# A planned attention-and-MLP kernel: fills by another rule, one conversion per weight tile, alpha of two chunks by itself

## The chip, the core and the metric

One core of a Trainium2 chip runs the whole program. It has five engines with a queue each: TensorE (PE; its weight loads are shown as PEld), VectorE (DVE), ScalarE (ACT), GpSimd (POOL) and SyncE (SP), which issues most DMAs. Each engine works through its instructions in order; semaphores hold an instruction until what it needs is done. The metric is the device time of one execution in microseconds, the median of three runs.

## The reference

```python
for t in range(S):                                   # B, H, S, D = 4, 8, 768, 48
    state = alpha[:, :, t, :, None] * state + einsum('bhd,bhe->bhde', k[:, :, t], v[:, :, t])
    y[:, :, t] = einsum('bhd,bhde->bhe', q[:, :, t], state)
x = y.transpose(0, 2, 1, 3).reshape(B * S, H * D)    # 3072 x 384
h = x @ w_in                                         # 384 x 2048, float64 words
g = h * tanh(log1p(exp(min(h, 20))))                 # h itself above 20 in the log
out = (g @ w_out).astype(float32)                    # 2048 x 384
```

## The kernel before

The sequence is cut into 24 chunks of 128 tokens (6 per batch, chunk `n` of batch `n % 4`). For each chunk, `attention(n)` forms running products of alpha by two scans on VectorE: `rest` (line 431, towards the chunk's end) and the front scan (line 443). K is multiplied by `rest`, Q by the front. TensorE then makes the scores (`sc`, line 467), VectorE masks them into `probs` (line 475), and TensorE makes the product `y` (line 490). For the state, TensorE transposes K (`kb`, line 596), ScalarE copies it (`ks`), and TensorE makes `u` (line 605). The result is split into a rounded upper and a lower part and stored in `xs`; for the first six chunks TensorE subtracts the upper part (`off`, line 522).

The MLP runs in units: a unit takes one tile of 128 of the 2048 middle columns (`f`) and 2 or 4 chunks, nine matmuls up (`h`, line 647), an activation on ScalarE and VectorE (`u`, `t`, `y`, `g`), and three matmuls down per chunk (`o`, line 711), which need `g`. Weights arrive as 64-bit words. `weight(f)` loads a tile of 768 KB (`ws`) and makes fp32 words of it on VectorE in three passes for each of its two halves: a first pass (line 311, shift and mask) and two bits passes (lines 316 and 321). ScalarE rounds the upper part (line 326); the lower is made by two TensorE matmuls (lines 343 and 344) for tiles 0 to 3, by GpSimd (line 329) for the others.

The order of the instructions is written out ahead by `Plan.order`: each task has an engine, a cost and a due time (`key`); at each step the engine takes, of its first 150 waiting tasks, the one that can begin earliest, and of equals the one with the smallest key. The instructions are then emitted in that order and never move again. Where TensorE has nothing to do at the start it runs fills: 70 matmuls on a tile of zeros, whose results nobody reads; they are tasks with the key 12.

At the end `good` is made of all checks (line 821). Only if a check fails does the general path run, a slow version of everything with loops.

Of the kernel before, what the change touches and what calls it, by code (L numbers as in the profile page):

```python
# [28 lines left out]
P = 128  # L29
# [57 lines left out]
class Plan:  # L87
# [21 lines left out]

    def order(self):  # L110
# [33 lines left out]
        while len(done) < n:  # L144
            best = None
            for e in ENGINES:
                first = None
                for t in waiting[e][:WINDOW]:
# [4 lines left out]
                    if first is None or r < first[0] - 1e-9:  # L153
                        first = (r, t)
                if first and (best is None or first[0] < best[0]):
                    best = first
            if best is None:
                raise ValueError("no task can begin: " + str([w[0].key for w in waiting.values() if w]))
            at, t = best
            e = t.engine  # L160
# [22 lines left out]
    "load part": (0.7, 3.3), "load q": (1.8, 5.0), "load v": (0.7, 4.0), "load w": (2.0, 5.0),  # L183
    "move": (0.63, 2.5), "store": (0.47, 3.0),
    "fill": (0.165, 0.2), "off": (0.4, 0.65), "w off": (0.95, 1.2), "lead": (0.27, 0.38), "bits": (0.47, 0.58), "w hi": (0.42, 0.56), "w lo": (0.95, 1.08),
# [3 lines left out]
    "scores": (1.1, 1.35), "y0": (1.1, 1.4), "y": (2.0, 2.25), "turn": (0.4, 0.65),  # L189
# [15 lines left out]
def fast_path(ctx, tc, qka, v, w, out, good):  # L205
# [73 lines left out]
    for n in reversed(range(n_chunks)):  # L279
        mine = first_unit[n] - LEAD  # L280
        due[n] = min(mine, due[n + 1] - SPREAD) if n + 1 < n_chunks else mine

# [7 lines left out]
    def weight(f):  # L290
        key = weight_unit[f] - W_LEAD
# [10 lines left out]
        fs = slice(f * P, (f + 1) * P)  # L302
        for m in range(2):
            hi, lo = (wo[:, z, f : f + 1, :] if m else wi[:, z, :, fs] for z in range(2))
            as_hi = lambda t, hi=hi: t.rearrange("p (s f) -> p s f", f=hi.shape[-1])
            lead = plan.buffer("lead")
            words = lambda z, m=m: stage.tile[:, m, :, z]

            def begin(m=m, lead=lead, words=words):
                new(lead, [P, DM], f"w_lead{f}_{m}", dtype=I32)  # L310
                nc.vector.tensor_scalar(
                    lead.tile, words(1), 3, 0x3FFFFFF8, ALU.logical_shift_left, ALU.bitwise_and
                )

            def signs(lead=lead, words=words):
                nc.vector.scalar_tensor_tensor(  # L316
                    lead.tile, words(1), -0x40000000, lead.tile, ALU.bitwise_and, ALU.bitwise_or
# [703 lines left out]
```

## Time and profile before

| | |
|---|---|
| median of 3 runs | 540.15 us (540.0 to 540.23) |
| the profiled execution | 541.82 us, its span 540.1 us |
| TensorE busy | 529.0 us (98%) |
| VectorE busy | 398.7 us (74%) |
| ScalarE busy | 398.0 us (74%) |
| GpSimd busy | 39.5 us (7%) |
| chain that ended last | PE 81%, DVE 10%, ACT 3%, DMA 3% |
| line 763, the fills | 70 matmuls, 2% of the chain |

The span is the time from the first to the last record of the profile; the execution's own time is longer by what lies around it. A share of busy time is a mean over stages with different limits. The chain follows the work back from the last instruction, at each step to what released it, or to the instruction ahead of it on its engine.

### The profile page before, as it was taken

Reading aid. Unit: us, or ns where it says so; the run is one execution under the profiler, and the core shown is the slowest. Engines: PE = TensorE matmul, PEld = TensorE weight load, DVE = VectorE, ACT = ScalarE, POOL = GpSimd, SP = SyncE. Lnnn points to the kernel's source line nnn. Section 1 sums busy time; section 2 is a strip of 40 time slices with the busy share of each in tenths; the row PEclk is TensorE's granted clock in tenths of the full one; section 3 lists DMA queues with packets and bytes.
Section 4 is the critical chain, followed back from the end, with each engine's and each line's share of the span. In section 5 each row is a group of like instructions: output and inputs, shape, how many; then the busy total and the mean of one; then the engine's idle time right before and its main releaser. Section 6 shows DMA issues by size and latency. Waiting matters only on the chain.

```text
span 540.1 us, 9382 instructions
## 1 busy us (share of the span) xinstructions
PE 529.0 (98%) x3382; PEld 466.9 (86%) x3382; DVE 398.7 (74%) x719; ACT 398.0 (74%) x910; POOL 39.5 (7%) x37
## 2 busy tenths in 40 slices
PE   8999999999999999999999999999999999999994
PEld 4778999989898888888899888889988899999994
DVE  6999999999998797668974458985457845454441
ACT  1577778898779998997967865557766567786772
POOL 2000204233342000000000000000000000000000
PEclk9999999999999999999999999999999999999998
DMA  8655626131443785466220122220032000000001
GB/s 255 189 170 175 195 75 185 64 118 59 132 170 124 233 274 182 138 207 213 74 73 2 58 74 74 74 74 2 17 110 77 13 7 1 26 34 1 1 0 64
DMA packets 21812, 54.20 MB, mean 100 GB/s; under 512 B 4000, under 2 KB 14752, under 8 KB 21760
## 3 DMA queue, kind: packets, MB, share of 16 engines
q1 hardware_dynamic: 21472, 53.45, 32.0%
q8 instruction: 28, 0.46, 0.4%
q14 instruction: 24, 0.20, 0.1%
q10 hardware_dynamic: 288, 0.10, 0.1%
HBM read 46.45 MB, written 4.72 MB: 95 GB/s over the span
## 4 chain that ended last, share of the span: by engine, by line
PE 81%; DVE 10%; ACT 3%; DMA 3%; issue 1%; SPq 0%; ACTq 0%; DVEq 0%
PE o L711 31%; PE h L647 31%; PE y L490 7%; PE sc L467 4%; PE u L605 3%; PE spare L763 2%; DVE t L674 2%; PE kb L596 2%; DMA wc<-in_wp_dram 1%; DVE g L681 1%; DMA qka<-in_qka_dram 1%; DVE y L665 1%; DVE w_lead L316 1%; DVE w_lead L321 1%; DVE rest L431 1%
## 5 line engine op out<-in xcount | busy, mean ns | idle before, releaser
L711 PE MATMUL o<-wo,g 128*128 128x384 f32 x1152 | 227.2, 342 | 0.3 <-DVE g L681 0.3
L647 PE MATMUL h<-xs,wi 128*128 128x512 f32 (+1 forms) x954 | 218.7, 374 | 0.6 <-POOL wi L329 0.3
L711 PEld LDWEIGHTS o<-wo,g 128*128 128x128 f32 x1152 | 202.0, 188 | 9.6 <-issue 1.0
L647 PEld LDWEIGHTS h<-xs,wi 128*128 128x128 f32 x954 | 166.8, 188 | 28.0 <-POOL wi L329 0.8
L655 ACT ACTIVATE u<-h 128x512 f32<-128x512 f32 (+1 forms) x106 | 58.6, 552 | 80.9 <-PE h L647 80.2
L681 DVE TENSOR_TENSOR g<-t,g 128x512 fp32r<-128x512 f32 (+1 forms) x106 | 68.1, 643 | 49.5 <-ACT g L678 49.1
L665 DVE SCALAR_TENSOR_TENSOR y<-u,h 128x512 f32<-128x512 f32 (+1 forms) x106 | 67.0, 633 | 49.4 <-ACT u L655 48.9
L674 DVE SCALAR_TENSOR_TENSOR t<-y,t 128x512 f32<-128x512 f32 (+1 forms) x106 | 69.5, 657 | 9.3 <-ACT t L671 9.0
L668 ACT ACTIVATE t<-t,tenth 128x512 f32<-128x512 f32 (+1 forms) x106 | 71.8, 677 | 2.0
L678 ACT ACTIVATE g<-t 128x512 fp32r<-128x512 f32 (+1 forms) x106 | 61.7, 583 | 9.8 <-DVE t L674 5.1
L661 ACT ACTIVATE t<-u 128x512 f32<-128x512 f32 (+1 forms) x106 | 62.5, 589 | 3.1 <-DVE g L681 0.6
L671 ACT ACTIVATE t<-t 128x512 f32<-128x512 f32 (+1 forms) x106 | 61.6, 581 | 0.7
L431 DVE TENSOR_TENSOR_SCAN rest<-qka,behind 112x516 f32<-112x516 f32 x24 | 30.9, 1286 | 9.6 <-DMA qka<-in_qka_dram 9.5
L475 DVE COPY_PREDICATED probs<-causal,sc 128x512 f32<-128x512 uint32 x48 | 33.1, 731 | 3.5 <-PE sc L467 3.4
L443 DVE TENSOR_TENSOR_SCAN qka<-qka,ahead 112x516 f32<-112x516 f32 x24 | 30.8, 1282 | 0.0
L467 PEld LDWEIGHTS sc<-qka 48*128 48x128 f32 x384 | 23.3, 187 | 6.7 <-issue 4.5
L329 POOL TENSOR_TENSOR wi<-w_lead,wi 128x384 fp32r<-128x384 f32 x12 | 19.8, 1651 | 114.6 <-ACT wi L326 114.6
L467 PE MATMUL sc<-qka 48*128 48x128 f32 x384 | 27.9, 285 | 0.0
L490 PE MATMUL y<-probs,v 128*64 128x128 f32 (+1 forms) x384 | 26.1, 278 | 0.0
L490 PEld LDWEIGHTS y<-probs,v 128*64 128x64 f32 (+1 forms) x384 | 20.3, 129 | 3.8 <-issue 0.7
L490 PEld LDWEIGHTS y<-qka,state 112*112 112x112 f32 x160 | 19.9, 176 | 1.8 <-DVE probs L475 0.5
L490 PE MATMUL y<-qka,state 112*112 112x128 f32 x160 | 20.9, 273 | 0.2 <-DVE probs L475 0.2
(83 smaller groups left out, 401.3 us busy)
## 6 DMA issues: line engine op xcount, KB each, us to landing
qka<-in_qka_dram SPq DMA_DIRECT2D x23, 674.2 KB, 5.1
ws<-in_wp_dram SPq DMA_DIRECT2D x16, 768.0 KB, 4.5
wc<-in_wp_dram SPq DMA_DIRECT2D x16, 768.0 KB, 4.7
v<-in_vp_dram SPq DMA_DIRECT2D x24, 192.0 KB, 3.3
out_dram<-osb SPq DMA_DIRECT2D x16, 192.0 KB, 1.9
xs<-x SPq DMA_DIRECT2D x138, 16.0 KB, 2.9
out_dram<-part SPq DMA_DIRECT2D x8, 192.0 KB, 2.7
qka<-in_qka_dram SPq DMA_DIRECT2D x2, 224.0 KB, 3.6
```

The lines of the kernel that those rows point to most:

```text
L467: nc.tensor.matmul(p[a][:, j], K()[r : r + D, j], Q()[r : r + D, j], start=True, stop=True)
L490: nc.tensor.matmul(o, l, r, start=m < (2 if first else 1), stop=m >= len(ops) - 2, skip_group_check=True,)
L647: nc.tensor.matmul(p[:, :N], wi[:, z, s, fs], x[:, a, s], start=m == 0, stop=m == len(passes) - 1)
L655: nc.scalar.activation(wide(u), wide(h), AF.Exp, scale=-1.0, accum_out=uchk[:, at : at + 1])
L661: nc.scalar.activation(wide(t), wide(u), AF.Square, bias=1.0, scale=2.0)
L665: nc.vector.scalar_tensor_tensor(wide(y), wide(u), 0.5, wide(h), ALU.add, ALU.mult)
L668: nc.scalar.activation(wide(t), wide(t), AF.Ln, bias=tenth, scale=0.1)
L671: nc.scalar.activation(wide(t), wide(t), AF.Exp, scale=-1.0)
L674: nc.vector.scalar_tensor_tensor(wide(t), wide(y), 0.4, wide(t), ALU.mult, ALU.mult)
L678: nc.scalar.activation(g.tile[:, 0, :N], wide(t), AF.Copy)
L681: nc.vector.tensor_tensor(g.tile[:, 1, :N], wide(t), g.tile[:, 0, :N].bitcast(F32), ALU.subtract)
L711: nc.tensor.matmul(o.tile, g.tile[:, a, j * C : (j + 1) * C], wo[:, z, f], start=begins and m == 0, stop=end and m == 2,)
```

## The change

The two halves of a weight tile are converted together: three VectorE passes of 768 columns instead of six of 384, in one buffer `lead` of twice the size. The rounding and the lower parts stay as two halves. For chunk 1, alpha is loaded by itself, one planned microsecond ahead of q and k, which come in one transfer; chunk 0 has three parts as before. The fills read the identity matrix instead of a zeroed tile. A fill is now planned only where TensorE would otherwise wait for longer than one lasts, and only up to a planned time of 26; what is left is dropped. Of 150, 56 are emitted (before: 70 of 70). They stand in runs: before 22 (to `kb` of chunk 0), 9 (to its scores), 12 (to its product), 6, 2, 6, 2, 10 and 1; now 10, 12, 11, 5, 2, 2, 3, 3 and 8. Some planned costs are new, and two tables of shifts are there, empty. In the general path the loop over the middle columns takes four tiles at a time and loads their weights anew for each 128 rows.

```diff
-FILLS = 70
-FILL_KEY = 12.0
+FILLS = 150
+IDLE, IDLE_UNTIL, IDLE_BANK = 12.34567, 26.0, "o3"
+PARTED = 2
+DUE_SHIFT = {}
+W_SHIFT = {}
-W_PE = 4
+W_PE = lambda f, m: f < 4
+STOP_AT = 1e9
...
-                    if first is None or r < first[0] - 1e-9:
+                    if t.key == IDLE:
+                        spare = spare or (r, t)
+                    elif first is None or r < first[0] - 1e-9:
                         first = (r, t)
+                if spare and spare[0] > IDLE_UNTIL:
+                    dropped = self.drop(waiting, free_slots)
+                elif spare and (first is None or first[0] > spare[0] + spare[1].cost):
+                    first = spare
...
-    "fill": (0.165, 0.2), "off": (0.4, 0.65), "w off": (0.95, 1.2), "lead": (0.27, 0.38), "bits": (0.47, 0.58), "w hi": (0.42, 0.56), "w lo": (0.95, 1.08),
+    "fill": (0.165, 0.2), "fill0": (0.33, 0.36),
+    "off": (0.34, 0.6), "w off": (0.84, 1.08), "lead": (0.47, 0.58), "bits": (0.87, 0.98),
...
+        lead = plan.buffer("lead")
+        words = lambda z: stage.tile[:, :, :, z]
+        def begin():
+            new(lead, [P, 2, DM], f"w_lead{f}", dtype=I32)
+            nc.vector.tensor_scalar(
+                lead.tile, words(1), 3, 0x3FFFFFF8, ALU.logical_shift_left, ALU.bitwise_and
+            )
...
+        bits = add("DVE", *COST["lead"], key, begin, [got], [stage, lead], port=True)
+        bits = add("DVE", *COST["bits"], key + 0.01, signs, [bits], [stage, lead], port=True)
+        bits = add("DVE", *COST["bits"], key + 0.02, ends, [bits], [stage, lead], port=True)
         for m in range(2):
...
-            t = add("DVE", *COST["lead"], k, begin, [got], [stage, lead], port=True)
-            t = add("DVE", *COST["bits"], k + 0.01, signs, [t], [stage, lead], port=True)
-            t = add("DVE", *COST["bits"], k + 0.02, ends, [t], [stage, lead], port=True)
-            a = add("ACT", *COST["w hi"], k + 0.03, upper, [t], [lead])
+            a = add("ACT", *COST["w hi"], k + 0.03, upper, [bits], [lead])
...
+        elif n < PARTED:
+            got_a, got_k = (
+                add("SP", *COST[z], key - Q_LEAD - early, load_part(*e), uses=[q_buf])
+                for z, e, early in (
+                    ("load part", (a_at, QKA), 1.0), ("load two", (0, a_at), 0.0)
+                )
+            )
+            got_q = got_k
...
-        nothing = const.tile([P, DM], BF16, name="nothing")
-        nc.vector.memset(nothing, 0.0)
+        some = ident.bitcast(BF16)[:, :P]
...
-            nc.tensor.matmul(spare.tile[:, :DM], nothing[:, :P], nothing, start=True, stop=True)
+            nc.tensor.matmul(
+                spare.tile[:, :DM].rearrange("p (j t) -> p j t", j=NK), some,
+                some.unsqueeze(1).broadcast_to([P, NK, P]), start=True, stop=True,
+            )
         for i in range(FILLS):
-            add("PE", *COST["fill"], FILL_KEY if i else -1e6, fill, uses=[spare])
+            cost = COST["fill" if i > 12 else "fill0"]
+            add("PE", *cost, IDLE if i else -1e6, fill, uses=[spare])
...
-            for f0 in range(0, NFF, 4):
+            with tc.For_i(0, NFF, 4) as f0:
+                wi = sb.tile([P, NK, 4 * P], F32, name="wi_g")
+                wo = sb.tile([P, 4, DM], F32, name="wo_g")
```

On SyncE, the transfers at the start, before: `qka_115` and `v_122` are chunk 0, `qka_129` and `v_144` chunk 1, `ws` the weight tiles 0 and 1.

```order
L409 DMA qka_115<-in_qka_dram 112x517
L409 DMA qka_115<-in_qka_dram 112x512 x2
L413 DMA v_122<-in_vp_dram 128x384
L404 DMA qka_129<-in_qka_dram 112x1541
L413 DMA v_144<-in_vp_dram 128x384
L296 DMA ws_153<-in_wp_dram 128x1536
L296 DMA ws_173<-in_wp_dram 128x1536
L404 DMA qka_217<-in_qka_dram 112x1541
```

The same place now: chunk 0 is `qka_113`, chunk 1 `qka_119`.

```order
L441 DMA qka_113<-in_qka_dram 112x517
L441 DMA qka_113<-in_qka_dram 112x512 x2
L441 DMA qka_119<-in_qka_dram 112x517
L445 DMA v_124<-in_vp_dram 128x384
L441 DMA qka_119<-in_qka_dram 112x1024
L445 DMA v_136<-in_vp_dram 128x384
L328 DMA ws_145<-in_wp_dram 128x1536
L328 DMA ws_159<-in_wp_dram 128x1536
L436 DMA qka_220<-in_qka_dram 112x1541
```

Alpha of chunk 1 stands ahead of the v of chunk 0, its q and k in the place of the whole transfer.

On VectorE, from the front scan of chunk 0 to the front scan of chunk 1, before (`rest_185` is the scan of chunk 1, line 475 the masks of chunk 0):

```order
L443 SCALAR_TENSOR_TENSOR qka_115<-qka_115,ahead 112x516
L453 TENSOR_TENSOR qka_115<-qka_115 112x512
L431 SCALAR_TENSOR_TENSOR rest_185<-qka_129,behind 112x516
L475 COPY_PREDICATED probs_91<-causal,sc_0_175 128x512
L475 COPY_PREDICATED probs_93<-causal,sc_1_176 128x512
L436 RECIPROCAL ahead<-rest_185 112x4
L439 TENSOR_TENSOR qka_129<-qka_129,rest_185 112x512
L443 SCALAR_TENSOR_TENSOR qka_129<-qka_129,ahead 112x516
```

The same now (`rest_151` is the scan of chunk 1, line 515 the masks of chunk 0):

```order
L483 SCALAR_TENSOR_TENSOR qka_113<-qka_113,ahead 112x516
L471 SCALAR_TENSOR_TENSOR rest_151<-qka_119,behind 112x516
L493 TENSOR_TENSOR qka_113<-qka_113 112x512
L476 RECIPROCAL ahead<-rest_151 112x4
L479 TENSOR_TENSOR qka_119<-qka_119,rest_151 112x512
L483 SCALAR_TENSOR_TENSOR qka_119<-qka_119,ahead 112x516
L515 COPY_PREDICATED probs_91<-causal,sc_0_169 128x512
L515 COPY_PREDICATED probs_93<-causal,sc_1_170 128x512
```

The scan of chunk 1 has moved ahead of the multiplication of q of chunk 0, and three more passes of chunk 1 ahead of the masks of chunk 0.

On VectorE, from the end of that stretch to the scan of chunk 2, before (`ws_153` is weight tile 0, `rest_286` the scan of chunk 2):

```order
L311 TENSOR_SCALAR w_lead_0_222<-ws_153 128x384
L453 TENSOR_TENSOR qka_129<-qka_129 112x512
L316 SCALAR_TENSOR_TENSOR w_lead_0_222<-ws_153,w_lead_0_222 128x384
L311 TENSOR_SCALAR w_lead_1_245<-ws_153 128x384
L321 SCALAR_TENSOR_TENSOR w_lead_0_222<-ws_153,w_lead_0_222 128x384
L316 SCALAR_TENSOR_TENSOR w_lead_1_245<-ws_153,w_lead_1_245 128x384
L475 COPY_PREDICATED probs_91<-causal,sc_0_234 128x512
L475 COPY_PREDICATED probs_93<-causal,sc_1_235 128x512
L321 SCALAR_TENSOR_TENSOR w_lead_1_245<-ws_153,w_lead_1_245 128x384
L431 SCALAR_TENSOR_TENSOR rest_286<-qka_217,behind 112x516
```

The same now (`ws_145` and `ws_159` are weight tiles 0 and 1, `rest_274` the scan of chunk 2):

```order
L493 TENSOR_TENSOR qka_119<-qka_119 112x512
L340 TENSOR_SCALAR w_lead_204<-ws_145 128x768
L340 TENSOR_SCALAR w_lead_206<-ws_159 128x768
L345 SCALAR_TENSOR_TENSOR w_lead_204<-ws_145,w_lead_204 128x768
L345 SCALAR_TENSOR_TENSOR w_lead_206<-ws_159,w_lead_206 128x768
L515 COPY_PREDICATED probs_91<-causal,sc_0_208 128x512
L515 COPY_PREDICATED probs_93<-causal,sc_1_209 128x512
L350 SCALAR_TENSOR_TENSOR w_lead_204<-ws_145,w_lead_204 128x768
L350 SCALAR_TENSOR_TENSOR w_lead_206<-ws_159,w_lead_206 128x768
L471 SCALAR_TENSOR_TENSOR rest_274<-qka_220,behind 112x516
```

Two whole weight tiles are converted ahead of the scan of chunk 2, where it was one.

## Rows read from the trace of the kernel before

**Rows 1.** Busy time by stretches: length, engines (instructions), granted clock, DMA share, GB/s.

```profile
0.00:10.00 10.00, 7.55 (x31) 4.03 (x32) 7.12 (x15) 2.09 (x4) 3.52 (x13) 1.00 0.82 227
...
35.00:60.00 25.00, 25.00 (x221) 22.04 (x220) 24.79 (x55) 20.54 (x60) 2.40 (x1) 1.00 0.59 176
...
100.00:165.00 65.00, 64.42 (x351) 57.46 (x350) 64.66 (x113) 54.37 (x116) 22.28 (x16) 1.00 0.33 110
```

**Rows 2.** Chain of waits, 0 to 30 us: start us, us, what.

```profile
2.45 6.57 PE spare L763 x22
...
9.41 1.46 PE spare L763 x9
...
11.96 2.06 PE spare L763 x12
...
15.04 1.08 PE spare L763 x6
...
16.39 0.34 PE spare L763 x2
...
18.78 0.98 PE spare L763 x6
```

**Rows 3.** Instructions in order of time, TensorE: start us, us, what, idle before.

```profile
2.45 6.57 PE L763 MATMUL spare<-nothing 128*128 128x384 bf16 x22 [2.45 <-DVE behind L240]
```

**Rows 4.** In order of time, weight loads of TensorE, 2 to 9 us.

```profile
2.74 0.15 PEld L763 LDWEIGHTS <-nothing 128*128 128x128 bf16 x1 [0.17 <-issue]
...
8.18 0.45 PEld L763 LDWEIGHTS <-nothing 128*128 128x128 bf16 x3 [0.17 <-issue]
```

**Rows 5.** In order of time, ScalarE.

```profile
2.72 0.31 ACT L230 ACTIVATE minus_ident<-ident 128x128 fp32r<-128x128 f32 x1 [0.62 <-POOL ident masks.py:199]
```

**Rows 6.** In order of time, VectorE, chunks 0, 1 and 3.

```profile
5.64 0.66 DVE L439 TENSOR_TENSOR qka<-qka,rest 112x512 f32<-112x512 f32 x1
...
7.48 0.69 DVE L453 TENSOR_TENSOR qka<-qka 112x512 f32<-112x512 f32 x1
9.37 1.23 DVE L431 TENSOR_TENSOR_SCAN rest<-qka,behind 112x516 f32<-112x516 f32 x1 [1.20 <-DMA qka<-in_qka_dram]
...
27.94 1.23 DVE L431 TENSOR_TENSOR_SCAN rest<-qka,behind 112x516 f32<-112x516 f32 x1 [1.09 <-DMA qka<-in_qka_dram]
```

**Rows 7.** DMA issues, 2.15 to 2.6 and 4 to 5 us: count, KB each, us to landing.

```profile
v<-in_vp_dram SPq DMA_DIRECT2D x1, 192.0 KB, 4.4
...
ws<-in_wp_dram SPq DMA_DIRECT2D x2, 768.0 KB, 8.7
```

**Rows 8.** In order of time, TensorE, products of chunks 0, 1 and 2.

```profile
13.95 1.09 PE L490 MATMUL y<-probs,v 128*64 128x128 f32 x16
...
19.68 1.09 PE L490 MATMUL y<-probs,v 128*64 128x128 f32 x16
...
27.95 1.09 PE L490 MATMUL y<-probs,v 128*64 128x128 f32 x16
```

**Rows 9.** In order of time, VectorE, passes of a weight tile.

```profile
23.95 0.35 DVE L311 TENSOR_SCALAR w_lead<-ws 128x384 int32<-128x384 int32 x1
24.21 0.55 DVE L321 SCALAR_TENSOR_TENSOR w_lead<-ws,w_lead 128x384 int32<-128x384 int32 x1
24.69 0.55 DVE L316 SCALAR_TENSOR_TENSOR w_lead<-ws,w_lead 128x384 int32<-128x384 int32 x1
```

**Rows 10.** Groups by shape, VectorE, 0 to 100 us: count, busy, mean ns, idle before.

```profile
L665 DVE SCALAR_TENSOR_TENSOR y<-u,h 128x256 f32<-128x256 f32 x20 | 8.3, 417 | 1.4 <-ACT u L655 1.1
```

**Rows 11.** In order of time, VectorE, the same line at double width.

```profile
525.40 0.69 DVE L665 SCALAR_TENSOR_TENSOR y<-u,h 128x512 f32<-128x512 f32 x1 [0.95 <-ACT u L655]
```

**Rows 12.** Chain of waits, 80 to 170 us: first and last VectorE pieces of a stretch.

```profile
88.03 0.43 DVE g L681
...
135.86 0.60 DVE g L681
```

**Rows 13.** In order of time, VectorE, the last row.

```profile
533.78 0.15 DVE L821 TENSOR_REDUCE good<-pf 1x1 int32<-1x7 f32 x1 [0.38 <-PE pf L820]
```

More of the change, by code (lines that the diff above doesn't have):

```diff
@@ L108, in add, with drop @@
         return t
+    def drop(self, waiting, free_slots):
+        left = [t for t in waiting["PE"] if t.key == IDLE]
+        waiting["PE"] = [t for t in waiting["PE"] if t.key != IDLE]
+        for t in left:
+            for u in t.uses:
+                u.left -= 1
+                if u.left == 0:
+                    free_slots[u.tag].append(u.free_at)
+                    free_slots[u.tag].sort()
+        return len(left)
     def order(self):
@@ L144, in order @@
         while len(done) < n:
-            best = None
+            best, dropped = None, 0
             for e in ENGINES:
-                first = None
+                first = spare = None
                 for t in waiting[e][:WINDOW]:
@@ L281, in fast_path @@
         due[n] = min(mine, due[n + 1] - SPREAD) if n + 1 < n_chunks else mine
+    for n, shift in DUE_SHIFT.items():
+        due[n] += shift
     ready_w = {}
     def weight(f):
-        key = weight_unit[f] - W_LEAD
+        key = weight_unit[f] - W_LEAD + W_SHIFT.get(f, 0.0)
         stage = plan.buffer("stage")
@@ L320, in ends @@
-            def ends(lead=lead, words=words):
-                nc.vector.scalar_tensor_tensor(
-                    lead.tile, words(0), 29, lead.tile, ALU.logical_shift_right, ALU.bitwise_or
-                )
-            def upper(lead=lead, hi=hi, as_hi=as_hi):
-                nc.scalar.activation(hi, as_hi(lead.tile.bitcast(F32)), AF.Copy)
-            def lower(lead=lead, hi=hi, lo=lo, as_hi=as_hi):
-                nc.gpsimd.tensor_tensor(
-                    lo, as_hi(lead.tile.bitcast(F32)), hi.bitcast(F32), ALU.subtract
-                )
@@ L342, in off @@
                     p = new(bank, [P, NPAIR * C], f"w{f}_{m}", ps)[:, :DM]
-                    nc.tensor.matmul(p, ident, lead.tile.bitcast(F32), start=True, stop=False)
+                    nc.tensor.matmul(p, ident, both(), start=True, stop=False)
                     nc.tensor.matmul(as_hi(p), minus_ident, hi, start=False, stop=True)
@@ L547, in attention @@
         last_front = t_front
-        t_k = add("DVE", *COST["mult"], key + 0.03, mult_k, [t_rest, got_k], [q_buf, rest], port=True)
+        t_k = add(
+            "DVE", *COST["mult"], key + 0.03, mult_k, [t_rest, got_k], [q_buf, rest], port=True
+        )
         t_q = add("DVE", *COST["mult"], key + 0.04, mult_q, [t_front, got_q], [q_buf], port=True)
@@ L923, in general_path @@
                 nc.vector.tensor_tensor(t, ph, t, ALU.mult)
+                po = ps.tile([P, DM], F32, name="po_g")
                 for i in range(4):
                     nc.tensor.matmul(
[L926 removed]
+                        po, t[:, i], wo[:, i], start=i == 0, stop=i == 3
                     )
[L928 to L929 removed]
+                nc.vector.tensor_tensor(o, po, o, ALU.add)
             nc.sync.dma_start(out[ds(r0, P), :], o)
```

67 lines of the change are left out of this document (36 added, 31 removed).

## The prediction

> **What bounds the kernel now.** I read the busy time by stretches first. From 35 us on TensorE is busy in every microsecond: 25.00 of 25.00 us, and still 64.42 of 65.00 us in the stretch in which VectorE is busiest (64.66) [rows 1]. Every useful matmul before has its counterpart after, so from there on the time is a fixed amount of TensorE work. What a change can give or take lies where TensorE does no useful work, which is nearly all ahead of 31 us. There the chain of waits shows it running the fills (`spare`, line 763) in six runs between the first attention steps [rows 2], and the start of the first fill shows 2.45 us of idle ahead of it [rows 3]. So I add up what is not useful before, do the same for the changed order, and take the difference.
>
> **Before.** Idle 2.45 us [rows 3]. The six runs of the chain are 6.57 + 1.46 + 2.06 + 1.08 + 0.34 + 0.98 = 12.49 us for 57 fills [rows 2]; 70 are issued in all (line 60). The 35 of the last five runs take 5.92 us, 0.169 us each, so the other 13 cost 13 x 0.169 = 2.20 us. Together 17.14 us.
>
> Why were the first 22 so long? Their weight loads start 0.32 us apart from 2.74 to 8.18 us; then three stand within 0.45 us [rows 4]. A fill moves 384 columns, and 384 in 0.32 us is 1.2 per ns: the lower of the two clock levels, although the granted clock reads 1.00 in the first 10 us too [rows 1]. 18 fills ran so, from 2.45 to about 8.2 us.
>
> **The change, part by part.**
>
> *The fills' operand.* The memset of `nothing` (line 758) goes; the fill reads `ident`, and ScalarE, which waits for the same tile from GpSimd, starts at 2.72 us [rows 5]. TensorE then begins at about 2.75 instead of 2.45: idle +0.30. The memset's place on VectorE saves nothing, since the cast behind it waits for GpSimd's mask. The same 384 columns pass.
>
> *The count and places of the fills.* Ahead of the first key transpose (`kb`) stand 10 fills where 22 stood, then 12 (9 before) up to the first scores, 11 (12) up to the first product, then 5, 2, 2, 3, 3 and 8: 56 in all. Ten at 0.32 end at 2.75 + 3.20 = 5.95. The transposes need the multiplication by `rest`, 5.64 + 0.66 = 6.30 [rows 6]: a wait of about 0.38. At the lower clock they take twice their 0.39 (the gap between 9.02 and 9.41 in [rows 2]), to 7.1: another 0.39. If the clock rises as before, at 8.2 to 8.4, four more fills run at 0.32 and the remaining 42 at 0.169. Not useful after: 2.75 + 3.20 + 0.38 + 0.39 + 1.28 + 7.10 = 15.10 us. I add 0.3 us for waits that the next parts leave, 15.4.
>
> *Alpha alone for chunk 1.* VectorE has stood idle for 1.20 us until the whole qka of chunk 1 landed, and scanned from 9.37 [rows 6]. Now alpha is the fourth transfer, in the place of v, which was issued at about 2.2 and took 4.4 us for 192 KB [rows 7]. For 226 KB I take 4.4 to 5.2 and so 6.6 to 7.4. The front scan of chunk 0 ends at 7.48 [rows 6], so this scan starts there, 1.9 us sooner. It stands ahead of the multiplication of q of chunk 0, which moves from 7.48 to about 8.73 and ends at 9.4; the scores of chunk 0, which wait for it, are not reached before 7.1 + 1.28 + 8 x 0.169 = 9.75 anyway, so it costs nothing while those fills stand there. The other part of chunk 1, a later issue behind the same bytes, should land at 9.4 to 9.9; then k (0.58) and the front scan (1.2) end at 11.2 to 11.7, the scores at 9.75 + 1.09 = 10.84, and the two masks at 12.5 to 12.9. The product of chunk 0 starts when 11 fills are through, 10.84 + 1.86 = 12.7, not 13.95 [rows 8]. SyncE gains one issue; its later issues are unchanged in order but for v, and move by about 0.45 us.
>
> *One conversion for both halves.* Six VectorE passes per weight tile become three of double width. Starts 0.26 behind a first pass and 0.48 behind a bits pass [rows 9] make 2 x (0.26 + 0.48 + 0.48) = 2.44 us a tile. Of the wide passes no row exists. Ends: at the least nothing beyond today's narrow passes (half, 1.22 us), at the most the full double, 2.44. I take a value near the double: `y` on VectorE takes 0.417 us for 256 elements and 0.69 for 512 [rows 10, 11], 1.07 ns per element, so 0.41 of the 0.48 us goes by the elements and 0.07 is fixed. Saving 0.07 of each pair gives 0.46 + 0.89 + 0.89 = 2.24, a saving of 0.2 a tile, 3.2 for 16. While TensorE is full this is worth nothing. But from 88 to 137 us nearly all pieces of the chain are VectorE's, passes of the weights among them [rows 12]: there VectorE must come forward by as much as TensorE, or the lead is lost. What moves is the order. After the q of chunk 1 (13.1) stand the first passes of two weight tiles and then the second passes: 0.46 + 0.46 + 0.89 + 0.89, with the second tile's load behind one more transfer (8.7 us at the median of the two [rows 7], the later one near 14.0). So the masks of chunk 1 run from 16.2 to 17.4, and its product follows at 17.5 (before 19.68 [rows 8]). Two third passes (1.78) end at 19.2, the scans of chunk 2 follow, its q at about 22.8, its scores on TensorE at 23.2 behind what stands there, its product at about 26.6. Before, that product started at 27.95 [rows 8]. In the stretch that follows the weight matmuls stand earlier by one group of 0.9 us, so the lead grows from 1.35 to about 1.9, near to what the sum gives. VectorE comes forward by more: its scan of chunk 3, at 27.94 before after 1.09 us of idle [rows 6], stands at about 26.9, with one narrow pass (0.48) and two wide ones (1.35) more behind it, 2.8 us of lead, and 0.2 a tile from there. So it holds in 88 to 137 us.
>
> *Without cost.* The new cost figures act through the order alone; the two shift tables are empty, the stop time is far away, and tiles 0 to 3 are still split on TensorE. The general path runs only if a check fails, and no row of its lines is in the trace. It still is code to be jumped over: between the last reduction, 533.78 + 0.15, and the end at 540.1 lie 6.2 us [rows 13]. No row shows the jump. As ends I take one transfer saved or added, 4.4 us at the most by the v of [rows 7], likelier under 2, and as value zero, since the long loops over VectorE stay.
>
> **The sum.** 17.14 - 15.4 = 1.74, and of the 0.58 us of idle in 100 to 165 us [rows 1], where VectorE now has the lead, I take 0.4 as gone: 2.14 us. The profiled execution took 541.82 us for a span of 540.1 us, 1.67 above the median of 540.15; its time would be 539.68, and the median 538.0.
>
> **A rule against this.** The row first: the slow fills last until 8.18, with TensorE busy from 2.45 [rows 4]. The Trainium skill (TensorE: Matmul & The Clock Gate, Part 1) states that the half clock is the default, that sustained activity releases it, and that the moment varies from run to run. The trace agrees that the first fills run at the half clock; whether a start at 2.75 with a gap at 5.95 delays the release no run here shows. By the rule it could come later than I assume; the second of the rivals prices this by rows.
>
> **The rivals.** *The convoy on VectorE.* With two tiles' passes ahead of the masks of chunk 1, a load that lands at 15.6 instead of 14.0 holds the masks up by 1.6 us; the product of chunk 1 is then at 19.1, and the gain of 2.14 shrinks to 0.5: 539.6, no change to speak of. For it: the load is the last of eight at the start, the slowest kind [rows 7]. Against it: VectorE arrives there only at 13.5.
>
> *The clock rises late.* If it stays low until 15.5 us, the scores of chunk 0 begin at 7.1 + 12 x 0.32 = 10.9 and last 2.2, seven fills run at 0.32 and four at 0.169, and the product is at 16.1, 2.1 later than before (13.95). Masks and products of chunk 1 follow at 20.6 (before 19.68), and with six more fills on the way to chunk 2 than there were, the end is 1.2 us late: 541.4. It decides from about 13 us. Against it: the three runs lie within 0.23 us of each other, so the rise does not wander much.
>
> *Long passes ahead of the gates.* From 88 to 137 us VectorE is the chain that ended last [rows 12]. A bits pass that is 0.40 us longer can hold up a gate step and so the matmuls that need it. If each of the eight tiles converted there held TensorE twice by 0.40, that is 6.4 us: 540.15 - 2.14 + 6.4 = 544.4, slower. It decides where TensorE's stock of ready matmuls is under 0.40 us; with half of the 16 at that, 541.2. Against it: 0.58 us of idle in 65 us says that the stock is nearly always there, and VectorE starts the stretch 2.8 us ahead.
>
> *The change does not do what it says:* fewer fills only bring back plain waits of the same length, since TensorE waits for the same scans. Then the loss before 31 us stays 17 us, and 540.1 results. Against it: the 1.20 us of idle on VectorE is real, and masks now wait for scans that begin 1.9 us sooner.
>
> **How the numbers follow.** My forecast with gains of 1.1 to 3.1 us (the upper end: no wait at all and the idle of the middle gone): 0.72. Convoy 0.10 and no effect 0.06, both within 0.2%, that is 1.08 us either way, what a measurement can tell. The late clock 0.04 and the long passes 0.08, slower in most of their cases. That is faster 0.72, same 0.17, slower 0.11. The forecast's own range is 537.0 to 539.1. Eight times in ten needs the convoy too, and below it a part of what the jump may save: 536.6 to 539.9.
>
> **What the new profile would show.** First fill at 2.75; ten slow ones; first scores near 9.8 and product near 12.7; the scan of chunk 1 near 7.5 with no wait for its load; the product of chunk 1 near 17.5 and of chunk 2 near 26.6; weight passes near 0.5 and 0.95 us each; TensorE full from 35 us. I am wrong if the fills stay slow past 10 us, if a wait for a weight load stands ahead of the masks of chunk 1, or if TensorE's idle between 60 and 300 us grows beyond 1.5 us.

## The result and the profile after

The changed kernel takes 544.52 us (median of 9 runs, 543.08 to 547.06), the kernel before 540.23 (9 runs beside them). The ratio is 1.0068, 95% interval 1.0049 to 1.0086: slower by 0.7%. The forecast of 538.0 and its range were wrong, and so was its sign. The profiled execution took 543.66 us for a span of 541.7.

In the profiled execution it went as forecast ahead of 31 us. TensorE in order of time (start us, us, what, idle before), against [rows 3, 8]:

```profile
2.74 3.38 PE L804 MATMUL spare<-ident 128*128 128x384 bf16 x10 [2.74 <-POOL ident masks.py:199]
6.36 0.99 PE L638 MATMUL kb<-ident,qka 112*128 112x112 f32 x4 [0.24 <-DVE qka L479]
7.16 2.13 PE L804 MATMUL spare<-ident 128*128 128x384 bf16 x12
...
12.21 1.10 PE L530 MATMUL y<-probs,v 128*64 128x128 f32 x16
...
16.89 1.09 PE L530 MATMUL y<-probs,v 128*64 128x128 f32 x16
...
26.13 1.09 PE L530 MATMUL y<-probs,v 128*64 128x128 f32 x16
```

Ten fills at the lower clock level, then the products of chunks 0, 1 and 2 at 12.21, 16.89 and 26.13 instead of 13.95, 19.68 and 27.95. But TensorE has no longer its full work behind that. Busy time by stretches, columns as in [rows 1], and the middle stretch of the kernel before as the last line:

```profile
35.00:60.00 25.00, 24.34 (x216) 21.45 (x215) 24.04 (x46) 17.85 (x57) 2.02 (x2) 1.00 0.53 162
60.00:100.00 40.00, 38.98 (x309) 36.47 (x309) 38.99 (x79) 33.19 (x102) 9.52 (x7) 1.00 0.44 135
100.00:165.00 65.00, 64.14 (x349) 57.43 (x348) 61.83 (x89) 55.13 (x121) 24.51 (x16) 1.00 0.37 123
...
60.00:100.00 40.00, 39.79 (x316) 37.61 (x315) 38.16 (x86) 32.09 (x100) 9.92 (x8) 1.00 0.43 126
```

TensorE is idle for 0.66 + 1.02 + 0.86 = 2.54 us between 35 and 165 us; before, 0.00 + 0.21 + 0.58 = 0.79. To see where the lead went I weighed every useful matmul by the usual distance from its start to the next and added them up to a given time. Against a second profile of the kernel before, the changed kernel is ahead by about 1.3 us at 35, 0.5 at 60 and 0.2 at 80; behind by 0.8 at 90, 1.4 at 120, 1.0 at 165 and 2.4 at 530.

**Where it is lost, first place: the moves of x of chunk 2.** SyncE's issues in order of time (`ws` a weight tile, `xs<-x` the moves, the first `ws` is tile 3, the second tile 4), and two lines of the kernel before, the moves and tile 4 behind them:

```profile
26.23 0.33 SPq L328 DMA_DIRECT2D ws<-in_wp_dram  x1
27.82 0.33 SPq L436 DMA_DIRECT2D qka<-in_qka_dram  x1
28.46 0.33 SPq L328 DMA_DIRECT2D ws<-in_wp_dram  x1
30.56 3.88 SPq L576 DMA_DIRECT2D xs<-x  x6
...
32.72 4.50 SPq L536 DMA_DIRECT2D xs<-x  x6
...
37.94 0.38 SPq L296 DMA_DIRECT2D ws<-in_wp_dram  x1
```

The tile whose load stood behind the moves before (37.94 us there) now stands ahead of them. DMA issues of the moves (count, KB each, median us to landing), now and before, and what ScalarE then waits for:

```profile
xs<-x SPq DMA_DIRECT2D x6, 16.0 KB, 6.3
...
xs<-x SPq DMA_DIRECT2D x6, 16.0 KB, 3.9
```

```profile
39.05 0.28 ACT L548 ACTIVATE x<-y 112x128 fp32r<-112x128 f32 x1 [1.06 <-DMA xs<-x]
```

A move of 16 KB takes 6.3 us to land (the six took 3.9 before), ScalarE stands 1.06 us, and TensorE loses 0.6 us there in this execution.

**Second place: gate pieces behind a weight pass that GpSimd holds up.** VectorE from 114 us, then GpSimd, ScalarE and TensorE at the same time:

```profile
114.57 1.37 DVE L340 TENSOR_SCALAR w_lead<-ws 128x768 int32<-128x768 int32 x1
115.87 0.34 DVE L498 TENSOR_TENSOR state<-state,rest 48x192 f32<-48x192 f32 x1
116.14 0.94 DVE L345 SCALAR_TENSOR_TENSOR w_lead<-ws,w_lead 128x768 int32<-128x768 int32 x1
117.00 0.68 DVE L723 TENSOR_TENSOR g<-t,g 128x512 fp32r<-128x512 f32 x1
```

```profile
114.06 1.47 POOL L366 TENSOR_TENSOR wo<-w_lead,wo 128x384 fp32r<-128x384 f32 x1
```

```profile
114.74 0.63 ACT L720 ACTIVATE g<-t 128x512 fp32r<-128x512 f32 x1 [0.43 <-DVE t L716]
```

```profile
117.74 0.44 PE L753 MATMUL o<-wo,g 128*128 128x384 f32 x1 [0.86 <-DVE g L723]
```

ScalarE has the upper half of the gate ready at 115.4. VectorE's lower half (L723) stands behind two passes of a weight tile and a small piece. The first pass takes 1.37 us, while the median for this line is 0.55: it started while GpSimd subtracted, and it ends 0.4 us after the subtraction does (115.94 and 115.53). So the gate piece starts at 117.0 and TensorE stands for 0.86 us. At 87.4 us the same happens behind a pass of 1.77 us:

```profile
85.22 1.77 DVE L345 SCALAR_TENSOR_TENSOR w_lead<-ws,w_lead 128x768 int32<-128x768 int32 x1
...
87.38 0.97 PE L753 MATMUL o<-wo,g 128*128 128x384 f32 x4 [0.50 <-DVE g L723]
```

The Trainium skill (SBUF — State Buffer, SBUF: two separate sides) states that VectorE and GpSimd share one pair of ports to the on-chip memory SBUF, and that whichever of a GpSimd instruction and a VectorE instruction of certain kinds (two inputs from SBUF, or a mode that uses both ports) starts first holds the pair to its end. The trace agrees: 43 VectorE pieces start during a subtraction, and 15 of them come out over 0.25 us longer, the longest by 0.85; none of the nine `y` pieces among the 43 does, whose input `h` is TensorE's output and not in SBUF. That the ports are the reason is what the skill states; the runs below show that the long pieces come and go with the subtractions. Over the whole kernel (min/median/max ns, first and last start):

```profile
L345 DVE SCALAR_TENSOR_TENSOR w_lead<-ws,w_lead x16: 933/950/1770, 13.7 to 147.6; 128x768 int32<-128x768 int32 x16
```

Between 35 and 166 us there are 15 VectorE pieces that took over 0.25 us more than the median of their kind, with 10.1 us more in all, each beside a subtraction. In both profiles of before it is 13 pieces with 9.4 us, each beside one too. The sum of the holds is hardly new; what stands behind them is.

**Third place: the end.** The last VectorE row:

```profile
534.74 0.15 DVE L866 TENSOR_REDUCE good<-pf 1x1 int32<-1x7 f32 x1 [0.38 <-PE pf L865]
```

From the end of this reduction to the end of the span it is 541.7 - (534.74 + 0.15) = 6.8 us; before it was 6.2 [rows 13].

### The profile page after: what moved, and what is told of

It reads as the page before. It is cut to its first block, busy times and chain, and to the rows that moved or that the text cites. A ratio compares the mean times of both kernels' runs of the same rounds, so it can differ in the third digit from the quotient of the medians.

```text
span 541.7 us, 9312 instructions
## 1 busy us (share of the span) xinstructions
PE 527.5 (97%) x3368; PEld 465.6 (86%) x3368; DVE 395.5 (73%) x670; ACT 397.0 (73%) x910; POOL 39.6 (7%) x37
## 4 chain that ended last, share of the span: by engine, by line
PE 79%; DVE 12%; ACT 3%; DMA 3%; issue 2%; SPq 1%; POOL 0%; DVEq 0%; ACTq 0%; POOLq 0%
PE o L753 33%; PE h L689 31%; PE y L530 6%; PE sc L507 4%; PE u L647 2%; DMA ws<-in_wp_dram 2%; DVE w_lead L345 1%; DVE probs L515 1%; PE kb L638 1%; DVE t L716 1%; DVE g L723 1%; DVE y L707 1%; DMA xs<-x 1%; PE spare L804 1%; DVE rest L471 1%
## 5 line engine op out<-in xcount | busy, mean ns | idle before, releaser
L723 DVE TENSOR_TENSOR g<-t,g 128x512 fp32r<-128x512 f32 (+1 forms) x106 | 68.4, 646 | 53.0 <-ACT g L720 52.5
L471 DVE TENSOR_TENSOR_SCAN rest<-qka,behind 112x516 f32<-112x516 f32 x24 | 29.5, 1231 | 12.7 <-DMA qka<-in_qka_dram 12.7
L483 DVE TENSOR_TENSOR_SCAN qka<-qka,ahead 112x516 f32<-112x516 f32 x24 | 29.7, 1236 | 0.0
```

The lines of the kernel that those rows point to most:

```text
L723: nc.vector.tensor_tensor(g.tile[:, 1, :N], wide(t), g.tile[:, 0, :N].bitcast(F32), ALU.subtract)
```

## The experiments

Ratios are to the kernel before, run beside it on the same chip. One thing holds for all of these runs: an edit that changes a task of the plan lets the planner write a new order, so that more may differ than the lines shown. Where the traces show that the order stayed, it is said.

**Undoing and doing parts.** Narrow passes back (the changed kernel with the conversion of before):

```diff
-lead.tile, words(1)  # 128x768, three passes a tile
+lead.tile, words(1)  # 128x384, three passes a half, own buffer and due time
```

> The changed kernel with the six narrow passes per weight tile back (fills, alpha and general path stay changed). Theory of the double-width passes (they stand ahead of gate steps on VectorE and bring weight loads forward): the 4 us lost go and the early lead of about 2 us stays, 538 to 539.5 us. Theory of the code that is jumped over or of the fills: still 543 to 545 us.

541.45 us, 1.0004 (0.9992 to 1.0017), between the two ranges that were expected. The loss is in the double-width conversion and the order that comes with it; but the rest gives no gain either.

The conversion alone, in the kernel before (the zero operand of the fills cut to 128 columns, read three times, to make room):

```diff
-COST lead 0.27, bits 0.47; six passes of 128x384
+COST lead 0.47, bits 0.87; three passes of 128x768
```

> The kernel before with only the conversion in one piece of double width (the zero tile of the fills is cut to 128 columns and read three times, for space). Theory of the double-width passes: 542.5 to 545 us, TensorE's idle between 35 and 165 us above 2 us (before: 0.8). Theory that the fills or the code cost the time: 539 to 540.5 us.

546.86 us, 1.0111 (1.0090 to 1.0132), more than the 542.5 to 545 expected. TensorE is idle for 1.85 us from 60 to 100 and 1.64 from 100 to 165, and for 2.20 us from 20 to 35 as well, where in the two profiles of before it was 0.19 and 0.74.

The general path alone, in the kernel before:

```diff
-for f0 in range(0, NFF, 4):
+with tc.For_i(0, NFF, 4) as f0:  # and the loads of wi, wo inside
```

> The kernel before with only the general path changed, which does not run. Theory of the jumped-over code: 540.9 to 541.5 us, with all of the growth between the last reduction and the end and outside the span (before: 6.2 and 1.7 us). Every other theory: 540.2 us, unchanged.

541.52 us, 1.0007 (0.9994 to 1.0019): not told from nothing by the time; but in its profile 7.1 us follow the last reduction. The order on VectorE, ScalarE and TensorE is that of before.

**The loads.** Tiles 4 and 5 of the changed kernel loaded behind the moves of x of chunks 2 and 4:

```diff
+w_load[4].behind += moves[2]
+w_load[5].behind += moves[4]
```

> The changed kernel with the loads of weight tiles 4 and 5 held behind the x moves of chunks 2 and 4, where they stood before. Theory that the early load of tile 4 delays these moves (7.5 us instead of 2.9), so ScalarE and then the gates, and that VectorE never makes it up: 541 to 542.5 us, x moves of chunk 2 landing in under 4 us, no wait of ScalarE for them. Theory that the order of the passes on VectorE costs it by itself: 543.5 to 545 us although the moves land early.

543.25 us, 1.0043 (1.0023 to 1.0063): about a third of the loss, between the two ranges expected and with an interval that overlaps the changed kernel's. The moves land in 3.5 us and ScalarE doesn't wait for them. But of the 670 VectorE instructions only 556 stand in the same sequence as in the changed kernel, so the load is not the only difference.

**Pass length or joint readiness.** Six narrow passes in the changed kernel's task; each half rounded after its own three, or both after all six:

```diff
-upper, [bits], [lead]
+upper, [halves[m]], [lead]   # split_half
+upper, halves, [lead]        # split_joint
```

> The changed kernel with the six half-width VectorE passes put back into its new task: they write the two halves of the one double-width buffer, and ScalarE's rounding of each half waits for the three passes of its own half. Buffers and keys stay as the change has them. Theory 1, pass length (a gate piece that becomes ready behind a 0.56 or 0.94 us pass waits longer than behind a 0.35 or 0.55 us one): the loss goes, 541.0 to 542.2 us, as with all of the conversion put back (541.45). Theory 2, half readiness (the upper and lower weight halves of a tile reach ScalarE, GpSimd and TensorE only when the whole tile has been converted): also 541.0 to 542.2. Theory 3, the loads (the single double-width buffer and one key for both halves bring the conversion and its loads forward into the moves of x): 543.5 to 545. TensorE idle 60 to 100 us 1.0 us or more under theory 3, under 0.8 under the others.

> As split_half, but the rounding of either half waits for all six passes of the tile. Theory 1, pass length: 541.0 to 542.2 us. Theory 2, half readiness: 543.5 to 545, as the changed kernel. Theory 3, the loads: 543.5 to 545 as well, and here weight tile 4 is issued ahead of the moves of x of chunk 2, as in the changed kernel. Only theory 1 has this one fast; split_half fast beside it slow speaks for theory 2.

541.96 us, 1.0025 (1.0007 to 1.0044), and 544.42 us, 1.0068 (1.0045 to 1.0091). Taken alone, that speaks for joint readiness and against the length of a pass. But the second also has the load of tile 4 ahead of the moves, as said, and pays for it. Its waits from 35 to 60 us (us, times, longest):

```profile
ACT x L555 <- DMA xs<-x: 5.4, 1, 5.4
```

So this pair doesn't part the two. The first has a stall of TensorE on a gate piece too (1.2 us at 117), narrow as its passes are.

Due times of tiles 4 to 15 later by two units:

```diff
-W_SHIFT = {}
+W_SHIFT = {f: 2.0 for f in range(4, NFF)}
```

> The changed kernel with the planner's due times of weight tiles 4 to 15 later by two units (a unit of the schedule is one ScalarE piece of the gates), so that the wide passes and their loads stand behind gate pieces that they stood ahead of; weight tile 4 is still loaded ahead of the moves of x of chunk 2. Theory 1, pass length: the passes are as long as before and as many, 543.5 to 545 us. Theory 2, half readiness: later weights make it worse, 544 to 546. Theory 3 in the form that conversion stands too early among the gates (it ends at 150 us and not at 165): 541.5 to 542.7.

543.10 us, 1.0042 (1.0025 to 1.0058); the stalls at 86 and 117 us stay. None of the three theories said 543.1. As a test of the due times it is weak: 663 of the 670 VectorE instructions stand in the same sequence as in the changed kernel. It does bear on the loads: tile 4 is still loaded ahead of the moves, which land in 5.2 us, but ScalarE doesn't wait for them, TensorE is not idle from 35 to 60 us, and the run is as far below the changed kernel as the one with the loads held.

A second profile of the kernel before:

> The kernel before, unchanged, for a second profile of it. If the clock's rise differs between executions, the first 22 fills take about 5.3 us here and the budget of time that is not useful comes to some 16 us, 1.2 less than the 17.14 us of the first profile; if it doesn't, the fills take 6.6 us again. The end from the last reduction to the end of the span, 6.2 us in the first profile: within 0.3 of that if the 0.6 to 0.9 us that the changed general path showed is its own, up to 7 if it is spread of the runs.

540.27 us. Its 22 first fills:

```profile
2.45 5.40 PE L763 MATMUL spare<-nothing 128*128 128x384 bf16 x22 [2.45 <-DVE behind L240]
```

5.40 us, not the 6.57 of [rows 2]. The fills stand 0.32 us apart up to about 5.8 us and 0.16 from there, where in the first profile that step came at 8.2: the clock rose 2.4 us sooner, which made the 22 fills 1.2 us shorter. The end took 6.2 us again.

**Wide only ahead of the gates, or only among them.**

```diff
+WIDE = lambda f: f < 4    # mixed; mixed_rev: f >= 4
```

> The changed kernel with the double-width conversion for weight tiles 0 to 3 alone (they are converted before the gates start); tiles 4 to 15 are converted as before, six narrow passes, each half with a buffer and due time of its own. Theory 1, the loss sits in the conversion among the gates (tiles 4 on) and the gain in the one ahead of them: the lead of TensorE's useful work that the changed kernel had at 35 to 50 us (1.35 us over the second profile of the kernel before) is kept, 539.5 to 541.0 us, at or just under the kernel before. Theory 2, any new order draws a few stalls of its own, wherever the wide passes are: 541.5 to 543.5. Theory 3, the wide conversion of the first tiles (weight loads crowding the moves of x) costs as well: over 542, with TensorE idle 20 to 60 us of 0.6 us or more.

> The reverse: narrow conversion for tiles 0 to 3, double width for tiles 4 to 15. Theory 1 (the loss sits in tiles 4 on): 543.5 to 545.5 us, as the changed kernel or worse, with the stalls of TensorE on gate pieces between 60 and 165 us. Theory 2 (any new order): 541.5 to 543.5, no different from the mixed kernel. Theory 3 (the first tiles): 541.0 to 542.

543.96 us, 1.0055 (1.0035 to 1.0074), and 544.87, 1.0081 (1.0057 to 1.0104). My theory 1 fell: the first was to be as fast as before; its time is in the range of theory 3, that the wide conversion of the first tiles costs as well. It again loads tile 4 ahead of the moves (ScalarE waits 1.13 us) and waits 0.7 us for one gate piece; the second waits 2.0 us in three places for the same line.

**Without the subtractions.** GpSimd's 24 subtractions for tiles 4 to 15 go, in both kernels; the low halves are read from tile f mod 4:

```diff
-b = add("POOL", *COST["w lo"], k + 0.04, lower, [a], [lead], port=True)
+b = a
-wo[:, z, f]
+wo[:, z, f % 4 if z else f]   # wi alike
```

> The changed kernel without GpSimd's 24 subtractions of tiles 4 to 15; where the products want the low half of such a tile they read that of tile f mod 4, so TensorE has the same instructions but the output is another. Fourteen to sixteen VectorE pieces between 35 and 166 us are some 0.7 us longer while a subtraction runs, 10 us in all, with or without the change. Theory P, the loss is made where such a stretched piece and a wide one stand together ahead of a gate piece: without the subtractions the two stalls at 87 and 117 us go and the loss with them, 539.5 to 541.5 us, and at most 0.1% above the kernel before that also lacks them. Theory Q, the loss comes from the order and the joint readiness alone: still 2.5 to 4 us above that kernel.

> The kernel before without the same 24 subtractions, as the partner of the run just above. TensorE is hardly idle in it between 35 and 300 us (0.8 us in its second profile), so there is little for it to gain: 539.5 to 541.2 us under either theory.

Changed 539.23 us, 0.9970 (0.9953 to 0.9987); before 539.56 us, 0.9973 (0.9955 to 0.9991). The difference of 0.7% is gone. But the order is another in both: of the changed kernel's 670 VectorE instructions 559 stand in the same sequence as with the subtractions, of the 719 before 549. So this pair shows that the wide passes can go without loss, not yet that the subtractions alone made it. The changed kernel without them, by stretches and for the same line of VectorE:

```profile
60.00:100.00 40.00, 39.92 (x319) 38.14 (x318) 39.63 (x86) 34.41 (x105) 0.00 (x0) 1.00 0.51 158
100.00:165.00 65.00, 65.00 (x355) 58.38 (x354) 53.10 (x85) 62.84 (x137) 0.00 (x0) 1.00 0.48 160
```

```profile
L345 DVE SCALAR_TENSOR_TENSOR w_lead<-ws,w_lead x16: 936/950/957, 15.7 to 130.4; 128x768 int32<-128x768 int32 x16
```

The wide passes are as many, and as long at the median, and in this order they cost TensorE nothing: the longest takes 0.957 us, not 1.77. TensorE's idle time falls from 1.88 to 0.08 us in these two stretches, VectorE's work from 100 to 165 by 8.7.

That run also made the low halves ready sooner. So the same with all of the work kept, each subtraction cut in three. The plan is the same here, and so is the order of all VectorE and ScalarE instructions in both kernels:

```diff
-nc.gpsimd.tensor_tensor(lo, lead, hi, ALU.subtract)      # 128x384
+for a, b in cuts: nc.gpsimd.tensor_tensor(lo[:, a, b], ...)  # 128x128
```

> The changed kernel with each of GpSimd's subtractions (128x384, 1.0 to 1.2 us at the least) issued as three of 128x128, in the same place; the order on all engines is otherwise the same and TensorE waits for the low halves as before. Theory P (the loss is made by VectorE pieces that wait while a subtraction runs): if the hold lasts as long as one GpSimd instruction, a stretched piece gets 0.2 to 0.4 us longer instead of 0.7, and the time comes to 540.5 to 542.5 us; the sum of the stretches between 35 and 166 us falls from 10 us to under 7. If the third instruction is held as long as the whole was, or each cut pays a fixed price, 544 to 546. Theory R (without the subtractions the low halves were ready sooner, and that alone gave the gain): the cuts change nothing, 543.5 to 545, even where the stretches fall.

> The kernel before with the same three cuts. Its TensorE is idle little, so under theory P it gains less than the changed kernel: 539.5 to 541.0 us. If each cut pays a fixed price: 541.5 to 543. Theory R: no change, 540.5 to 541.5.

Changed 543.05 us, 1.0038 (1.0021 to 1.0055); before 540.43, 0.9986 (0.9961 to 1.0010). The changed kernel by stretches:

```profile
60.00:100.00 40.00, 39.61 (x324) 36.70 (x323) 39.15 (x79) 32.88 (x100) 13.91 (x20) 1.00 0.50 152
100.00:165.00 65.00, 64.90 (x354) 58.01 (x354) 62.47 (x94) 56.81 (x126) 39.82 (x48) 1.00 0.37 124
```

Idle 0.49 us instead of 1.88, and the stretched pieces cost 6.4 us instead of 10.1. In the changed kernel TensorE waits for gate pieces twice in these stretches (us in all, times, longest):

```profile
PE o L753 <- DVE g L723: 1.4, 2, 0.9
```

With the cuts, in the same order, it waits for none. The low halves don't come sooner either: GpSimd is busy for 53.7 us from 60 to 165 us, not 34.0. So it is the length of the hold that makes the waits at 87 and 117 us (theory P), and neither the order alone nor early low halves. The time shows less: it lies between the two ranges, 1.5 us under the changed kernel, and the two intervals still overlap. The profiled execution took 544.66 us and came to 60 us 2.5 us behind that of the changed kernel, which by itself gives VectorE more room; the pair with the loads held, below, has the same result from starts 0.6 us apart.

**What is left.** Both remedies at once, without and with the subtractions:

> The changed kernel without GpSimd's 24 subtractions (low halves of tiles 4 to 15 read from tile f mod 4) and with the loads of weight tiles 4 and 5 issued behind the moves of x of chunks 2 and 4. If the two causes, the load ahead of the moves and the VectorE pieces stretched by the subtractions, are the whole loss, the early gain of the change is left: 1.0 to 1.5 us below the kernel before without subtractions (539.56), 538.0 to 538.6 us. If the load costs nothing by itself: 539.0 to 539.5, as without the hold (539.23). If the change has no gain of its own: 539.3 to 540.

> The changed kernel complete, with both remedies: the loads of weight tiles 4 and 5 behind the moves of x, and each subtraction issued as three of 128x128. By the sum of the two measured alone (-1.3 and -1.4 us from 544.5): 541.5 to 542.2 us. If the remedies meet the same stalls: 542.8 to 543.3. If the stretches are all that is left beside the early gain: 540.0 to 541.0, at the kernel before.

539.50 us, 0.9983 (0.9967 to 0.9999), and 541.81, 1.0025 (1.0008 to 1.0042). The remedies add up, as expected of the second. Its order is that of the run with the loads held and whole subtractions (543.25); TensorE's idle time from 60 to 165 us falls from 1.55 to 0.20 us between the two, and the time by 1.4. But without subtractions holding the loads gives nothing (539.23 without the hold), and the first shows no gain of the change's own, though TensorE is not idle at all from 35 to 300 us. Its last VectorE row, under the line that gives the span:

```profile
core 0 of [0], span 537.9 us
...
531.12 0.15 DVE L871 TENSOR_REDUCE good<-pf 1x1 int32<-1x7 f32 x1 [0.38 <-PE pf L870]
```

6.6 us follow the reduction. In the 13 profiles with the changed general path it is 6.6 to 7.1 (mean 6.80), in the seven with the old one 5.2 to 6.2 (mean 5.77). Only that path put back, the order otherwise the same:

> As held_nopool (no subtractions on GpSimd, low halves of tiles 4 to 15 read from tile f mod 4, the loads of tiles 4 and 5 held), with the general path as it stood before. In 13 profiles of kernels with the changed general path 6.6 to 7.1 us lie between the end of the last reduction and the end of the span, in five with the old one 5.2 to 6.2. If the code that is jumped over makes that: 5.2 to 6.2 us here and 538.2 to 538.9 us in all, 0.7 to 1.2 under the kernel before without subtractions (539.56), which is the early gain of the change. If it isn't the code: 6.6 us or more and 539.2 to 539.8.

538.62 us, 0.9942 (0.9922 to 0.9962):

```profile
core 0 of [0], span 537.2 us
...
531.27 0.15 DVE L871 TENSOR_REDUCE good<-pf 1x1 int32<-1x7 f32 x1 [0.38 <-PE pf L870]
```

5.8 us follow. By the time it is 0.9 us under the kernel before without subtractions (539.56), by the ratios 0.3%, which is 1.7 us. The two intervals overlap a little and the orders differ, so a gain of the change's own is likely; its size is not shown.

A complete version, with the fills and alpha of the change, narrow passes, the old general path and the cuts:

> What the runs speak for, complete: the fills and their places, the early alpha and the new cost figures of the change; six narrow passes per weight tile as before; the general path as before; each subtraction on GpSimd issued as three of 128x128. From the run with the narrow passes back (541.45, the same as before): 1 us less by the old general path and 0.5 to 0.8 less by the cuts, 539.4 to 540.4 us, some 0.2 to 0.3% under the kernel before. If the early part has no gain that lasts and the code is not the tail: 540.5 to 541.5.

540.95 us, 0.9995 (0.9979 to 1.0011): no gain, in the lower of the two outcomes expected, although its end is short (5.8 us). TensorE is idle for 1.14 us from 60 to 100 us in it. No complete version here beats the kernel before for certain.

## Why the prediction was wrong, step by step

**Right, in the profiled execution.** The early chain: first fill 2.74 (2.75), ten slow fills 3.38 us (3.20), scan of chunk 1 at 7.36 with no wait for its load (7.5), products at 12.21, 16.89 and 26.13 (12.7, 17.5, 26.6). Wide passes of 0.55, 0.95 and 0.95 us; VectorE's work in all fell by 398.7 - 395.5 = 3.2 us, as summed. The sum of 1.74 was about right as a lead in this execution, 1.3 to 1.8 us at 35 us against the two profiles of before.

**Luck in it.** Part of the lead was the late clock of the one profile of before. The products came 0.5 to 0.6 us ahead of the forecast since the forecast let the clock rise at 8.2 to 8.4 us and four more fills run at 0.32 us, while in fact all fills from 7.16 us on stand 0.16 to 0.19 us apart. And the loads came early in this execution. Eight other profiles, of the runs above whose wide conversion takes in tiles 0 to 3, have the same order on VectorE up to 42 us and on SyncE up to 28 us. In each of them VectorE waits 0.68 to 1.41 us for the load of the second weight tile ahead of the masks of chunk 1; here the two first passes in the profile above, and in the run with loads held:

```profile
12.68 1.13 DVE L340 TENSOR_SCALAR w_lead<-ws 128x768 int32<-128x768 int32 x2
...
14.15 0.56 DVE L341 TENSOR_SCALAR w_lead<-ws 128x768 int32<-128x768 int32 x1 [0.70 <-DMA ws<-in_wp_dram]
```

In six of the eight it also waits 0.26 to 1.00 us for q and k of chunk 1. That is the rival "The convoy on VectorE" with its sign, and it got 0.10. The product of chunk 2 starts at 26.46 to 28.59 us in the eight; in five profiles with the early order of before it starts at 26.63 to 27.95. Weighed as above, the lead at 35 us over the mean of these five is 0.9 us on average over the nine, from -1.3 to 1.8: about half of the 1.74 of the sum.

One step of the working does not add up: a lead of 1.35 and one group of 0.9 us is 2.25, not "about 1.9"; the sum doesn't use it.

**Wrong: "it holds in 88 to 137 us".** This is the step that failed. VectorE did arrive early (scan of chunk 3 at 26.36, forecast 26.9). And "nearly all pieces of the chain are VectorE's" there is too much: VectorE has 37.3 of its 48.9 us, ScalarE 7.4. But what TensorE needs is not VectorE's mean lead; it is the next gate piece, and that waits for what stands ahead of it in VectorE's fixed order. Two such waits cost TensorE 1.4 us. I saw the stretch as full of ready matmuls because 0.58 us of idle stood in 65. A full row of busy time doesn't show how little is in stock. The rival "Long passes ahead of the gates" had the place and, with 544.4, nearly the time; it got 0.08. Its mechanism was short of one thing: the 0.40 us a pass alone did not stall TensorE, neither without subtractions (0.08 us of idle from 60 to 165, in another order) nor, on the gate pieces, with the subtractions cut in the same order. In the changed kernel it took a pass held up by GpSimd to push a gate piece past TensorE's stock. The subtractions were in [rows 1], 16 instructions and 22.28 us of GpSimd beside VectorE's 64.66, and I didn't ask what they do to VectorE.

**Wrong: the moves of x.** I followed weight loads as far as VectorE's waits for them, not what they do to small transfers issued behind them. By the run that held them that is 0.25% of the 0.68%; but this run has another order, the run with later due times got as much with the load still ahead, and without subtractions the hold gave nothing. The wait of ScalarE is shown, its share of the loss is not.

**Wrong: the code jumped over, "as value zero".** It is 1.0 us by the profiles (6.80 - 5.77), inside the ends that were named, and it takes back what the early gain is on average.

**Wrong: the rise of the clock.** "the rise does not wander much": the fills of before took 6.57 us in one profile and 5.40 in the other.

My named sign, TensorE idle over 1.5 us between 60 and 300 us, came true: 1.02 + 0.86 + 0.03 = 1.91.

**Open.** The changed kernel loses a further 1.4 us between 165 and 530 us against the second profile of before, 0.6 against the first. TensorE is idle for only 0.3 us of it; I did not follow where the rest goes. The cuts in the same order gave back 1.5 of the 4.3 us and the end took 1.0; the rest is not assigned by any run that kept the order. Which pieces meet a subtraction is set by the order as a whole: seven other orders with whole subtractions came out 0.25 to 1.1% slower, one (narrow passes back) did not, and I could not have named the places from the order alone. By the time alone, the joint readiness of both halves is not parted from the load of tile 4.

## What to carry to other kernels

Where one engine feeds another just in time, judge an edit by the longest run of work that can stand ahead of a needed piece, not by the sum of work saved: 3.2 us less on VectorE came with 4.3 us more in all here. A chain of waits read from one profile is one execution: look at a second before building on the times at which loads land or the clock rises. Look for pairs of engines whose instructions lengthen each other (compare the longest with the median of a line) before making either's pieces longer. And a change of order moves transfers too: check which small transfer now follows a large one.

## What the runs showed of the hardware

Of the 43 VectorE pieces that start during a GpSimd subtraction of 128x384 in the changed kernel, 15 take over 0.25 us more than usual, 0.7 us on average (10.1 us in all); without subtractions no piece between 35 and 166 us is that long in either kernel. The kernel before is 0.27% faster without them, in another order. Code that is never run lengthened the end of the program by 1.0 us. A 16 KB move behind a 768 KB load took 6.3 us to land instead of 3.9.
